# Scores product and fold in two token halves, the maximum ordered between products, new in-order positions, and down weights in row pairs, in a one-core decode block

## The chip, the cores and the metric

The kernel runs on one core of one Trainium2 chip. The metric is device time in microseconds (us) of one execution, smaller is better. The executions of one kernel on one chip agree within about 0.3%; the median over the runs is quoted.

Engines in the profile: PE (TensorE, matrix products; PEld is its weight load), DVE (VectorE), ACT (ScalarE), POOL (GpSimd), SP (SyncE, which here issues all large DMA loads). A "ring" below is one of the 16 parallel streams over which one DMA load is spread. Packet records in the trace show 16 packets in flight at a time.

## The reference, cut to what matters

One decode token passes through an adaLN-conditioned block: layer norm, attention over a key and value cache of 32 heads with 16384 tokens of 128 elements, and then a gated feed-forward part.

```python
q = (h @ wq).reshape(32 heads, 128)
scores = einsum('bhqd,bhkd->bhqk', q, k_cache) * 128 ** -0.5      # 32 x 16384
p = softmax(scores, axis=-1)
o = einsum('bhqk,bhkd->bhqd', p, v_cache)
x = x + ga * (o.reshape(...) @ wo)
h = layernorm(x) * (1 + cb) + sb
x = x + gb * ((silu(h @ w_gate) * (h @ w_up)) @ w_down)           # 640 -> 1728 -> 640
# ... the modulation vectors sa, ca, ga, sb, cb, gb come from silu(c) @ w_mod
```

Each K or V head is 4 MB, so the two caches are 268 MB of the 291 MB that must be read. Nothing is read twice.

## The kernel before

All work is planned as operations with an engine, a position and dependencies. An engine executes its operations in the order of position, strictly. The scores of one head are made without a transposed K: DVE multiplies K (tokens on partitions and along the row) by a broadcast q in place, adds the two halves of the 128 elements ("fold1", 64 left), PE adds those up further against an identity matrix ("fold", 4 left), and DVE reduces the rest.

```python
o_mult[h]  = op(DVE, base, ...)          # kslot[128, 128 tokens, 128] *= q; 128x16384
o_fold1[h] = op(DVE, base + 8.8, ...)    # f1 = kslot[:, :, 0:64] + kslot[:, :, 64:128]
o_fold[h]  = op(PE, base + 13.5, ...)    # 16 products of 512 columns, S_ps = sum over groups of GC = 4
o_red[h]   = op(DVE, base + 17.0, ...)   # S_sb = sum over the last 4
o_max[h]   = op(DVE, base + 19.3, ...)   # pm = max over the row
o_gm[h]    = op(POOL, base + 19.6, ...)  # maximum over partitions
# ... nb, exp on ACT; the next head's product has position base + 20 and waits for nothing but K and q
o_pvlast[h] = op(PE, vbase, f_pv, deps=[o_exp[h], d_v[h][0], ...])   # V product
```

The loads: K and V have two buffers each. K of head h+2 is issued when `fold1` of head h is done; V of head h when the V product of head h-2 is done. All are issued in one fixed order by SP, the last ones being V of head 30, V of head 31 (four pieces), the gate, up and down weights.

```python
vdeps = [o_pvlast[h - 2]] if h >= 2 else [...]
wd_src = B_wd[0:128 * FJ, :].rearrange("(j p) n -> p j n", p=128)   # rows of 640 x 2 B = 1280 B
wd_cut = [(0, 5), (5, 9), None, (9, FJ - 1), (FJ - 1, FJ)]           # five loads, None: the 64 last rows
```

## Time and profile before

| | before |
|---|---|
| median | 690.39 us (690.14 to 691.23, 4 runs) |
| span of the profiled run | 688.9 us |
| bytes read | 290.96 MB, 422 GB/s over the span |
| busy | DVE 66%, PE 49%, POOL 43%, ACT 12%; DMA 90% or more in all slices but the last |

In the profile's lines, kring and vring are the buffers of K and V, f is the result of `fold1`, psb is PSUM (the memory that PE writes its products to), gm is the maximum over partitions, and SPq is SP issuing loads.

From the page of the profile of the kernel before: busy time of the engines; then the span in 40 slices with the DMA's busy tenths and its GB/s; then the chain of work that ended last.

```profile
PE 336.4 (49%) x3320; PEld 173.8 (25%) x3320; DVE 454.4 (66%) x155; ACT 85.3 (12%) x308; POOL 292.9 (43%) x75
...
DMA  9999999999999999999999999999999999999997
GB/s 383 418 427 436 438 433 425 432 428 430 429 425 436 437 430 429 431 430 427 432 433 427 431 429 434 429 434 431 430 427 422 431 440 436 425 426 430 390 370 263
...
DMA 37%; DVE 21%; POOL 18%; PE 17%; SPq 3%; ACT 2%; issue 1%
DMA kring<-in_A_k_cache_dram 36%; POOL gm L439 18%; DVE kring L419 13%; PE psb L429 9%; PE psb L458 7%; DVE f L421 6%; SPq L71 3%; DVE S_sb L433 2%; DMA kring<-in_B_w_down_dram 1%; ACT P_sb L443 1%; DVE pm L436 1%; ACT R_sb L407 1%; PE psb 
```

The DMA row says that the queue is full nearly everywhere, and the GB/s row that it moves about 430 in the middle. A kernel with no hole at 430 GB/s would need 677 us for its bytes. What can be won lies mainly in the start and the last three slices. POOL has 18% of the chain with its maximum (`gm`), although it should be a tiny operation.

From the timeline of the kernel before: one head near the end, where DVE does not wait for K. The columns are start, duration, engine, line, operation, and in brackets the idle time before it with what ended it.

```profile
583.38 8.68 DVE L419 TENSOR_TENSOR kring<-kring,qbc_sb 128x16384 bf16<-128x16384 bf16 x1
583.56 8.72 POOL L439 PARTITION_ALL_REDUCE gm<-pm  x1 [6.33 <-DVE pm L436]
597.29 3.63 PE L429 MATMUL psb<-f,ident 128*128 128x512 bf16 x16
...
600.96 0.69 DVE L433 TENSOR_REDUCE S_sb<-psb 128x128 f32<-128x512 f32 x1 [4.43 <-PE psb L429]
...
601.88 8.68 DVE L419 TENSOR_TENSOR kring<-kring,qbc_sb 128x16384 bf16<-128x16384 bf16 x1
```

The next head's product starts on DVE at 583.38, POOL's maximum 0.2 us later, and POOL ends when the product ends: 8.72 us. The cycle from product to product is 601.88 - 583.38 = 18.5 us here, up to 20.1 in later heads, and 19.2 on average over the last five cycles (product starts from 545.4 to 641.4). A head's K and V need 8.39 MB / 430 GB/s = 19.5 us.

Busy time of each engine in short stretches of the kernel before. The last two columns are the DMA's busy share and GB/s; the one ahead of them is the TensorE clock that the throttle granted (1.00 is full).

```profile
core 0: us, PE busy (x) PEld busy (x) DVE busy (x) ACT busy (x) POOL busy (x), PEclk, DMA share, GB/s
651.00:652.00 1.00, 0.69 (x10) 0.42 (x14) 1.00 (x1) 0.25 (x3) 0.81 (x1) 0.50 0.76 328
652.00:653.00 1.00, 1.00 (x16) 0.46 (x12) 1.00 (x1) 0.00 (x0) 1.00 (x1) 0.50 0.53 229
653.00:654.00 1.00, 1.00 (x16) 0.33 (x12) 1.00 (x1) 0.00 (x0) 1.00 (x1) 0.50 0.30 131
654.00:655.00 1.00, 1.00 (x12) 0.16 (x4) 0.59 (x1) 0.14 (x1) 0.83 (x1) 0.51 0.38 164
655.00:656.00 1.00, 1.00 (x9) 0.43 (x6) 0.00 (x0) 0.78 (x3) 0.00 (x0) 1.00 0.00 0
656.00:657.00 1.00, 1.00 (x6) 0.44 (x5) 0.00 (x0) 0.00 (x0) 0.00 (x0) 1.00 0.76 147
```

This is a hole in the load stream. The last V load is issued at 655.2 us, when the V product of head 29 has ended; that product began at 651.60, right after an exponential that waited for a maximum of 8.7 us (641.62 to 650.33). From the timeline: that exponential (P_sb), the scaled output of a head (On), its output product, the V product, and the last V load.

```profile
650.61 0.40 ACT L443 ACTIVATE P_sb<-S_sb,nb 128x128 bf16<-128x128 f32 x1
...
651.01 0.24 ACT L497 ACTIVATE On<-psb,rl 128x1 bf16<-128x1 f32 x1
...
651.31 0.36 PE L505 MATMUL psb<-On,woring 128*128 128x1 bf16 x5 [10.04 <-ACT On L497]
...
651.60 3.56 PE L458 MATMUL psb<-vring,P_sb 128*32 128x512 bf16 x32
...
655.20 1.99 SPq L71 DMA_DIRECT2D vring<-in_A_v_cache_dram  x4
```

### The profile page before, as it was taken

The numbers are of one execution on the slowest core, as the hardware profiler recorded it, in microseconds if no ns is written. First come the engines' busy times: TensorE is split into PE (matmuls) and PEld (weight loads), VectorE is DVE, ScalarE is ACT, GpSimd is POOL, SyncE is SP. The second block draws the span as 40 slices with busy tenths as digits, with TensorE's granted clock in tenths as the row PEclk, the third lists the DMA queues.
The fourth block names the chain that finished last, engine by engine and source line by source line (L and its number), as shares of the span: only waits on it lengthen the run. The fifth ranks groups of instructions, "written<-read, shape, count | busy, mean of one in ns | idle before, by whom it ended". The sixth has DMA issues, their size and how long they took to land.

```text
span 688.9 us, 7385 instructions
## 1 busy us (share of the span) xinstructions
PE 336.4 (49%) x3320; PEld 173.8 (25%) x3320; DVE 454.4 (66%) x155; ACT 85.3 (12%) x308; POOL 292.9 (43%) x75
## 2 busy tenths in 40 slices
PE   1503455565444445655444455643446256544484
PEld 1501222232122222322122222311223122212253
DVE  0077767667788776656787666667766676778801
ACT  0100101111111111111011111101111011111010
POOL 0006666556677654324055531000054365667600
PEclk9997666667676666667666666666666666766675
DMA  9999999999999999999999999999999999999997
GB/s 383 418 427 436 438 433 425 432 428 430 429 425 436 437 430 429 431 430 427 432 433 427 431 429 434 429 434 431 430 427 422 431 440 436 425 426 430 390 370 263
DMA packets 13613, 290.96 MB, mean 422 GB/s; under 512 B 1354, under 2 KB 3596, under 8 KB 4492
## 3 DMA queue, kind: packets, MB, share of 16 engines
q1 hardware_dynamic: 13576, 290.48, 98.7%
q8 instruction: 26, 0.43, 0.2%
q14 instruction: 7, 0.06, 0.0%
q10 hardware_dynamic: 4, 0.00, 0.0%
HBM read 290.47 MB, written 0.00 MB: 422 GB/s over the span
## 4 chain that ended last, share of the span: by engine, by line
DMA 37%; DVE 21%; POOL 18%; PE 17%; SPq 3%; ACT 2%; issue 1%
DMA kring<-in_A_k_cache_dram 36%; POOL gm L439 18%; DVE kring L419 13%; PE psb L429 9%; PE psb L458 7%; DVE f L421 6%; SPq L71 3%; DVE S_sb L433 2%; DMA kring<-in_B_w_down_dram 1%; ACT P_sb L443 1%; DVE pm L436 1%; ACT R_sb L407 1%; PE psb L410 0%; ACT nb L441 0%; ACT On L497 0%
## 5 line engine op out<-in xcount | busy, mean ns | idle before, releaser
L419 DVE TENSOR_TENSOR kring<-kring,qbc_sb 128x16384 bf16<-128x16384 bf16 x32 | 278.0, 8687 | 28.6 <-DMA kring<-in_A_k_cache_dram 28.6
L439 POOL PARTITION_ALL_REDUCE gm<-pm x32 | 145.1, 4534 | 319.2 <-DVE pm L436 314.2
L458 PE MATMUL psb<-vring,P_sb 128*32 128x512 bf16 x992 | 109.0, 618 | 126.3 <-DMA vring<-in_A_v_cache_dram 126.3
L446 POOL PARTITION_ALL_REDUCE Ls<-rs x32 | 145.0, 4532 | 27.4 <-ACT P_sb L443 27.4
L429 PE MATMUL psb<-f,ident 128*128 128x512 bf16 x512 | 132.1, 414 | 27.8 <-DVE f L421 27.5
L421 DVE TENSOR_TENSOR f<-kring 128x8192 bf16<-128x8192 bf16 x32 | 141.6, 4424 | 1.1
L433 DVE TENSOR_REDUCE S_sb<-psb 128x128 f32<-128x512 f32 x32 | 22.1, 691 | 153.5 <-PE psb L429 153.5
L429 PEld LDWEIGHTS psb<-f,ident 128*128 128x128 bf16 x512 | 50.1, 103 | 117.3 <-DVE f L421 42.1
L458 PEld LDWEIGHTS psb<-vring,P_sb 128*32 128x32 bf16 x992 | 33.7, 138 | 179.8 <-DMA vring<-in_A_v_cache_dram 128.5
L410 PE MATMUL psb<-R_sb,ones_bf 128*128 128x128 bf16 x32 | 8.5, 266 | 126.5 <-ACT R_sb L407 126.5
L478 PEld LDWEIGHTS psb<-sel,acc_sb 128*32 128x32 f32 (+1 forms) x920 | 58.9, 157 | 13.8 <-issue 11.9
L478 PE MATMUL psb<-sel,acc_sb 128*32 128x1 f32 (+1 forms) x920 | 61.2, 200 | 0.7 <-ACT acc_sb L463 0.7
L441 ACT ACTIVATE nb<-gm 128x1 f32<-128x1 f32 x32 | 6.5, 203 | 313.3 <-POOL gm L439 313.3
L410 PEld LDWEIGHTS psb<-R_sb,ones_bf 128*128 128x128 bf16 x32 | 3.3, 104 | 129.5 <-ACT R_sb L407 129.5
L463 ACT ACTIVATE acc_sb<-psb 128x512 f32<-128x512 f32 x31 | 18.5, 596 | 108.8 <-PE psb L458 108.7
L505 PE MATMUL psb<-On,woring 128*128 128x1 bf16 x160 | 8.1, 180 | 41.7 <-ACT On L497 41.7
L448 ACT ACTIVATE lnl<-Ls 128x1 f32<-128x1 f32 x32 | 6.5, 202 | 112.7 <-POOL Ls L446 112.7
L505 PEld LDWEIGHTS psb<-On,woring 128*128 128x128 bf16 x160 | 7.3, 131 | 42.6 <-ACT On L497 42.6
L443 ACT ACTIVATE P_sb<-S_sb,nb 128x128 bf16<-128x128 f32 x32 | 12.8, 402 | 1.2 <-ACT nb L441 0.2
L407 ACT ACTIVATE R_sb<-ident,q_r 128x128 bf16<-128x128 bf16 x32 | 12.7, 397 | 0.6
L413 ACT ACTIVATE qbc_sb<-psb 128x128 bf16<-128x128 f32 x32 | 8.9, 277 | 14.2 <-PE psb L410 14.2
L328 POOL PARTITION_ALL_REDUCE st<-st x2 | 0.8, 392 | 21.7 <-DVE x L529 11.4
(72 smaller groups left out, 88.1 us busy)
## 6 DMA issues: line engine op xcount, KB each, us to landing
kring<-in_A_k_cache_dram SPq DMA_DIRECT2D x32, 4096.0 KB, 25.1
vring<-in_A_v_cache_dram SPq DMA_DIRECT2D x31, 4096.0 KB, 33.0
wreg<-in_A_wq_dram SPq DMA_DIRECT2D x1, 5120.0 KB, 26.6
woring<-in_A_wo_dram SPq DMA_DIRECT2D x8, 640.0 KB, 24.8
vring<-in_w_mod_dram SPq DMA_DIRECT2D x1, 4800.0 KB, 14.6
vring<-in_A_v_cache_dram SPq DMA_DIRECT2D x4, 1024.0 KB, 9.4
wreg<-in_B_w_gate_dram SPq DMA_DIRECT2D x1, 2160.0 KB, 16.5
wreg<-in_B_w_up_dram SPq DMA_DIRECT2D x1, 2160.0 KB, 21.4
```

The lines of the kernel that those rows point to most:

```text
L71: return e.dma_start(out_ap, in_ap)
L407: o_R[h] = op(ACT, base - 15.0 if h > 0 else 2.5, lambda e, h=h, s2=s2: e.activation(out=R_sb[:, s2], in_=ident[:], func=ACTF.Copy, scale= ...
L419: o_mult[h] = op(DVE, base, lambda e, kslot=kslot, qb=qb: e.tensor_tensor(out=kslot, in0=kslot, in1=qb, op=ALU.mult), deps=[d_k[h], o_qbc[ ...
L421: o_fold1[h] = op(DVE, base + 8.8, lambda e, kslot=kslot: e.tensor_tensor(out=f1[:], in0=kslot[:, :, 0:64], in1=kslot[:, :, 64:128], op=AL ...
L429: r = e.matmul(S_ps[s2][:].rearrange("p (t r) -> p t r", r=GC), lhsT=ident[:], rhs=f1[:, :, GC * m:GC * (m + 1)], start=(m == 0), stop=(m ...
L433: o_red[h] = op(DVE, base + 17.0, lambda e, s2=s2: e.tensor_reduce(out=S_sb[:, s2], in_=S_ps[s2][:].rearrange("p (t r) -> p t r", r=GC), a ...
L439: o_gm[h] = op(POOL, base + 19.6, lambda e, h=h: e.partition_all_reduce(gm[:, h:h + 1], pm[:, h:h + 1], channels=128, reduce_op=bass.bass_ ...
L443: o_exp[h] = op(ACT, base + 20.4, lambda e, h=h, s2=s2, sp=sp: e.activation(out=P_sb[:, sp, 0:TT], in_=S_sb[:, s2], func=ACTF.Exp, scale=S ...
L446: o_L[h] = op(POOL, base + 21.0, lambda e, h=h: e.partition_all_reduce(Ls[:, h:h + 1], rs[:, h:h + 1], channels=128, reduce_op=bass.bass_i ...
L458: r = e.matmul(acc_ps[s2][q4:q4 + 32, :], lhsT=P_sb[:, sp, 4 * j:4 * j + 32], rhs=vring[:, s2, 4 * j:4 * j + 4, :].rearrange("p a d -> p ( ...
L463: o_acc[h] = op(ACT, vbase + 9.0, lambda e, s2=s2: e.activation(out=acc_sb[:, s2, :], in_=acc_ps[s2][:], func=ACTF.Copy), deps=[o_pvlast[h ...
L478: r = e.matmul(dst, lhsT=blk, rhs=sel[:, i:i + 1], start=(i == 0), stop=(i == 3))
```

## The change

Its intent: shorten the head's cycle and take the maximum out of the collision with the product. The product and `fold1` are made in two halves of 64 tokens, so that PE folds the first half while DVE multiplies the second; each half has its own bank of PSUM and leaves 8 values (GC = 8) for the reduction; the products of the next head wait for the maximum; small operations of ACT and PE get earlier positions; the down weights come in pairs of neighbouring rows (2560 B), for which the gate and up weights are picked at a stride of two columns.

```diff
-    GC = 4
+    GC = 8
+    NH = 2
-            vbase = base + 10.5 + PERIOD * lead(h)
+            vbase = base + 10.0 + PERIOD * lead(h)
-            o_mult[h] = op(DVE, base, ... 128x16384 ..., deps=[d_k[h], o_qbc[h]])
-            o_fold1[h] = op(DVE, base + 8.8, ...)
-            o_fold[h] = op(PE, base + 13.5, f_fold, ...)
-            o_red[h] = op(DVE, base + 17.0, ...)
+            for c in range(NH):
+                o_mult[h] = op(DVE, base + 6.5 * c, ... 128x8192 ...,
+                               deps=[d_k[h], o_qbc[h], o_gm[h - 1] if h >= 1 else None])
+                o_fold1[h] = op(DVE, base + 6.5 * c + 4.4, ...)
+                o_fold[h].append(op(PE, base + 6.5 * c + 6.7, f_fold, ...))      # 8 products of 512 columns
+                reds.append(op(DVE, base + 15.0 + c, ...))                       # 128x512 -> 128x64
 # ... max, gm, nb, exp, L, lnl, rl: positions about 2 earlier; acc, diag, on, wo: 5 to 6 earlier
+        NPR = FJ // 2
+        wd_cut = [(0, 3), (3, 5), None, (5, NPR), NPR]                            # in row pairs
+                src = B_wd[256 * c[0]:256 * c[1], :].rearrange("(q p i) n -> p q (i n)", p=128, i=2)
 # ... gate and up: w = wv[:, k, 256 * (j // 2):...].rearrange("p (m i) -> p i m", i=2)[:, j % 2, :]
```

More of the change, by code (lines that the diff above doesn't have):

```diff
@@ L215, in build @@
         acc_sb = sb("acc_sb", [128, 2, 512], F32)
-        sel = sb("sel", [128, GC], F32)
+        sel = sb("sel", [128, 4], F32)
         identf = sb("identf", [128, 128], F32)
@@ L271, in build @@
         o_sel = op(DVE, 0.1, lambda e: e.tensor_reduce(
-            out=sel[:], in_=ident[:].rearrange("p (g r) -> p r g", g=4)[:, 0:GC, :], axis=AX.X, op=ALU.add), deps=[o_ident], name="sel")
+            out=sel[:], in_=ident[:].rearrange("p (g r) -> p r g", g=4)[:, 0:4, :], axis=AX.X, op=ALU.add), deps=[o_ident], name="sel")
         o_idf = op(DVE, 0.12, lambda e: e.tensor_copy(out=identf[:], in_=ident[:]), deps=[o_ident], name="identf")
@@ L380, in build @@
         o_R, o_qbcmm, o_qbc = [None] * H, [None] * H, [None] * H
-        o_fold = [None] * H
+        o_fold = [[] for _ in range(H)]
         o_mult, o_fold1, o_red, o_max = [None] * H, [None] * H, [None] * H, [None] * H
@@ L415, in build @@
                 deps=[o_qbcmm[h], o_mult[h - 2] if h >= 2 else None], name="qbc%d" % h)
-            kslot = kring[:, s2]
-            qb = qbc_sb[:, s2].unsqueeze(1).broadcast_to([128, TT, 128])
-            o_mult[h] = op(DVE, base, lambda e, kslot=kslot, qb=qb: e.tensor_tensor(out=kslot, in0=kslot, in1=qb, op=ALU.mult),
-                           deps=[d_k[h], o_qbc[h]], name="mult%d" % h)
-            o_fold1[h] = op(DVE, base + 8.8, lambda e, kslot=kslot: e.tensor_tensor(
-                out=f1[:], in0=kslot[:, :, 0:64], in1=kslot[:, :, 64:128], op=ALU.add),
-                deps=[o_mult[h], o_fold[h - 1] if h >= 1 else None], name="fold1_%d" % h)
@@ L425, in f_fold @@
-            def f_fold(e, s2=s2):
-                r = None
-                n = 64 // GC
-                for m in range(n):
-                    r = e.matmul(S_ps[s2][:].rearrange("p (t r) -> p t r", r=GC), lhsT=ident[:], rhs=f1[:, :, GC * m:GC * (m + 1)],
-                                 start=(m == 0), stop=(m == n - 1))
-                return r
-            o_fold[h] = op(PE, base + 13.5, f_fold, deps=[o_fold1[h], o_ident, (o_modc_a, o_qbf)[h] if h < 2 else o_red[h - 2]], name="fold%d" % h)
@@ L433, in build, with f_fold @@
-            o_red[h] = op(DVE, base + 17.0, lambda e, s2=s2: e.tensor_reduce(
-                out=S_sb[:, s2], in_=S_ps[s2][:].rearrange("p (t r) -> p t r", r=GC), axis=AX.X, op=ALU.add),
-                deps=[o_fold[h], o_exp[h - 2] if h >= 2 else None], name="red%d" % h)
-            o_max[h] = op(DVE, base + 19.3, lambda e, h=h, s2=s2: e.tensor_reduce(
+            TH = TT // NH
+            qb = qbc_sb[:, s2].unsqueeze(1).broadcast_to([128, TH, 128])
+            reds = []
+            for c in range(NH):
+                ks = kring[:, s2, c * TH:(c + 1) * TH, :]
+                f1h = f1[:, c * TH:(c + 1) * TH, :]
+                sh = S_ps[c][:].rearrange("p (t r) -> p t r", r=GC)
+                o_mult[h] = op(DVE, base + 6.5 * c, lambda e, ks=ks, qb=qb: e.tensor_tensor(out=ks, in0=ks, in1=qb, op=ALU.mult),
+                               deps=[d_k[h], o_qbc[h], o_gm[h - 1] if h >= 1 else None], name="mult%d_%d" % (h, c))
+                o_fold1[h] = op(DVE, base + 6.5 * c + 4.4, lambda e, ks=ks, f1h=f1h: e.tensor_tensor(
+                    out=f1h, in0=ks[:, :, 0:64], in1=ks[:, :, 64:128], op=ALU.add),
+                    deps=[o_mult[h], o_fold[h - 1][c] if h >= 1 else None], name="fold1_%d_%d" % (h, c))
+                def f_fold(e, sh=sh, f1h=f1h):
+                    r = None
+                    n = 64 // GC
+                    for m in range(n):
+                        r = e.matmul(sh, lhsT=ident[:], rhs=f1h[:, :, GC * m:GC * (m + 1)], start=(m == 0), stop=(m == n - 1))
+                    return r
+                o_fold[h].append(op(PE, base + 6.5 * c + 6.7, f_fold, deps=[o_fold1[h], o_ident, (o_modc_a, o_qbf)[c] if h < 1 else o_red[h - 1]],
+                                    name="fold%d_%d" % (h, c)))
+                reds.append(op(DVE, base + 15.0 + c, lambda e, s2=s2, sh=sh, c=c: e.tensor_reduce(
+                    out=S_sb[:, s2, c * TH:(c + 1) * TH], in_=sh, axis=AX.X, op=ALU.add),
+                    deps=[o_fold[h][c], o_exp[h - 2] if h >= 2 else None], name="red%d_%d" % (h, c)))
@@ L437, in build @@
+            o_red[h] = reds[-1]
+            o_max[h] = op(DVE, base + 17.0, lambda e, h=h, s2=s2: e.tensor_reduce(
                 out=pm[:, h:h + 1], in_=S_sb[:, s2], axis=AX.X, op=ALU.max), deps=[o_red[h]], name="max%d" % h)
-            o_gm[h] = op(POOL, base + 19.6, lambda e, h=h: e.partition_all_reduce(
+            o_gm[h] = op(POOL, base + 17.3, lambda e, h=h: e.partition_all_reduce(
                 gm[:, h:h + 1], pm[:, h:h + 1], channels=128, reduce_op=bass.bass_isa.ReduceOp.max), deps=[o_max[h]], name="gm%d" % h)
-            o_nb[h] = op(ACT, base + 20.2, lambda e, h=h: e.activation(
+            o_nb[h] = op(ACT, base + 18.0, lambda e, h=h: e.activation(
@@ L442, in build @@
                 out=nb[:, h:h + 1], in_=gm[:, h:h + 1], func=ACTF.Copy, scale=-SCALE), deps=[o_gm[h]], name="nb%d" % h)
-            o_exp[h] = op(ACT, base + 20.4, lambda e, h=h, s2=s2, sp=sp: e.activation(
+            o_exp[h] = op(ACT, base + 18.2, lambda e, h=h, s2=s2, sp=sp: e.activation(
                 out=P_sb[:, sp, 0:TT], in_=S_sb[:, s2], func=ACTF.Exp, scale=SCALE, bias=nb[:, h:h + 1], accum_out=rs[:, h:h + 1]),
                 deps=[o_nb[h], o_red[h], o_pvlast[h - NP] if h >= NP else o_zp], name="exp%d" % h)
-            o_L[h] = op(POOL, base + 21.0, lambda e, h=h: e.partition_all_reduce(
+            o_L[h] = op(POOL, base + 18.6, lambda e, h=h: e.partition_all_reduce(
@@ L447, in build @@
                 Ls[:, h:h + 1], rs[:, h:h + 1], channels=128, reduce_op=bass.bass_isa.ReduceOp.add), deps=[o_exp[h]], name="L%d" % h)
-            o_lnl[h] = op(ACT, base + 30.2, lambda e, h=h: e.activation(
+            o_lnl[h] = op(ACT, base + 28.0, lambda e, h=h: e.activation(
                 out=lnl[:, h:h + 1], in_=Ls[:, h:h + 1], func=ACTF.Ln), deps=[o_L[h]], name="lnl%d" % h)
-            o_rl[h] = op(ACT, base + 30.3, lambda e, h=h: e.activation(
+            o_rl[h] = op(ACT, base + 28.1, lambda e, h=h: e.activation(
@@ L462, in build @@
                 o_pvlast[h] = op(PE, vbase, f_pv, deps=[o_exp[h], d_v[h][0], o_acc[h - 2] if h >= 2 else (o_xf, o_modc)[h], o_cc], name="pv%d" % h)
-                o_acc[h] = op(ACT, vbase + 9.0, lambda e, s2=s2: e.activation(out=acc_sb[:, s2, :], in_=acc_ps[s2][:], func=ACTF.Copy),
+                o_acc[h] = op(ACT, vbase + 3.0, lambda e, s2=s2: e.activation(out=acc_sb[:, s2, :], in_=acc_ps[s2][:], func=ACTF.Copy),
                               deps=[o_pvlast[h], o_diag[h - 2] if h >= 2 else None], name="acc%d" % h)
@@ L479, in f_diag @@
                     return r
-                o_diag[h] = op(PE, vbase + 9.5, f_diag, deps=[o_acc[h], o_sel, o_on[h - 1] if h >= 1 else None], name="diag%d" % h)
+                o_diag[h] = op(PE, vbase + 4.0, f_diag, deps=[o_acc[h], o_sel, o_on[h - 1] if h >= 1 else None], name="diag%d" % h)
             else:
@@ L496, in build @@
                 on_dst, on_src, on_sc = On[qs, h - hq:h - hq + G], OT_ps[qs, h - hq:h - hq + G], rl[qs, h:h + 1]
-            o_on[h] = op(ACT, vbase + 10.0, lambda e, a=on_dst, b=on_src, c=on_sc: e.activation(out=a, in_=b, func=ACTF.Copy, scale=c),
+            o_on[h] = op(ACT, vbase + 5.0, lambda e, a=on_dst, b=on_src, c=on_sc: e.activation(out=a, in_=b, func=ACTF.Copy, scale=c),
                          deps=[o_diag[h], o_rl[h]], name="on%d" % h)
@@ L508, in build @@
             if lastg:
-                o_wo[h] = op(PE, vbase + 10.5, lambda e, h=h: f_wo(e, h, h + 1), deps=[o_on[h], d_wo[h // G], o_gbr], name="wo%d" % h)
+                o_wo[h] = op(PE, vbase + 5.5, lambda e, h=h: f_wo(e, h, h + 1), deps=[o_on[h], d_wo[h // G], o_gbr], name="wo%d" % h)
             elif hq == G - 1:
-                o_wo[h] = op(PE, vbase + 10.5, lambda e, h=h: f_wo(e, h + 1 - G, h + 1), deps=[o_on[h], d_wo[h // G], o_gbr], name="wo%d" % h)
+                o_wo[h] = op(PE, vbase + 5.5, lambda e, h=h: f_wo(e, h + 1 - G, h + 1), deps=[o_on[h], d_wo[h // G], o_gbr], name="wo%d" % h)
         TE = T0 + (H - 1) * PERIOD + 10.5 + PERIOD * lead(H - 1) + 20.0
@@ L516, in build @@
         d_wu = plan.dma(QE + 0.01, wu_v, B_wu.rearrange("(p k) n -> p k n", k=KC), "wu", deps=[o_qmm], name="dma_wu")
-        wd_src = B_wd[0:128 * FJ, :].rearrange("(j p) n -> p j n", p=128)
-        wd_cut = [(0, 5), (5, 9), None, (9, FJ - 1), (FJ - 1, FJ)]
+        NPR = FJ // 2
+        wd_cut = [(0, 3), (3, 5), None, (5, NPR), NPR]
         d_wd = []
@@ L521, in build @@
             if c is None:
-                d_wd.append(plan.dma(QE + 0.02 + 0.01 * n, wdr_v[0:FR], B_wd[128 * FJ:F, :], ("wd", n), deps=[o_fold1[H - 2]], name="dma_wd%d" % n))
-            else:
-                d_wd.append(plan.dma(QE + 0.02 + 0.01 * n, wd_v[:, c[0]:c[1]], wd_src[:, c[0]:c[1]], ("wd", n), deps=[o_fold1[H - 2]], name="dma_wd%d" % n))
+                dst, src = wdr_v[0:FR], B_wd[128 * FJ:F, :]
+            elif c == NPR:
+                dst, src = wd_v[:, 2 * NPR, :], B_wd[256 * NPR:128 * FJ, :]
+            else:
+                dst = wd_v[:, 2 * c[0]:2 * c[1], :].rearrange("p (q i) n -> p q (i n)", i=2)
+                src = B_wd[256 * c[0]:256 * c[1], :].rearrange("(q p i) n -> p q (i n)", p=128, i=2)
+            d_wd.append(plan.dma(QE + 0.02 + 0.01 * n, dst, src, ("wd", n), deps=[o_fold1[H - 2]], name="dma_wd%d" % n))
         o_abf = op(ACT, TE, lambda e: e.activation(out=attn_bf[:], in_=attn_ps[:, 0:KC], func=ACTF.Copy), deps=[o_wo[H - 1]], name="attn_bf")
@@ L537, in build @@
                   deps=[o_t2], name="h2_col")
-        o_zg = op(DVE, TE - 1.0, lambda e: e.memset(g_ps[:, 0:FCH], 0.0), deps=[o_modc_a, o_red[H - 2]], name="zero_g")
+        o_zg = op(DVE, TE - 1.0, lambda e: e.memset(g_ps[:, 0:FCH], 0.0), deps=[o_modc_a, o_red[H - 1]], name="zero_g")
         o_zu = op(DVE, TE - 0.9, lambda e: e.memset(u_ps[:, 0:FCH], 0.0), deps=[o_qbf, o_red[H - 1]], name="zero_u")
@@ L545, in f_gu @@
                 for k in range(KC):
-                    w = wv[:, k, 128 * j:min(F, 128 * (j + 1))]
+                    if j < 2 * NPR:
+                        w = wv[:, k, 256 * (j // 2):256 * (j // 2 + 1)].rearrange("p (m i) -> p i m", i=2)[:, j % 2, :]
+                    else:
+                        w = wv[:, k, 128 * j:min(F, 128 * (j + 1))]
                     r = e.matmul(ps_t[0:(128 if j < FJ else FR), j:j + 1], lhsT=w, rhs=h2_col[:, k:k + 1],
@@ L582, in build @@
         for n, c in enumerate(wd_cut):
-            js = [FJ] if c is None else list(range(*c))
+            js = [FJ] if c is None else ([2 * NPR] if c == NPR else list(range(2 * c[0], 2 * c[1])))
             o_dn = op(PE, TE + 1.8 + 0.01 * n, lambda e, n=n, js=js: f_down(e, js, n == 0, n == len(wd_cut) - 1),
```

## The prediction

> **What bounds it now.** DMA. The page gives 290.96 MB in 688.9 us. In the table by 10 us stretches, every stretch from 10 to 650 us has a DMA share of 0.97 to 1.05 and about 430 GB/s; the packet records show 16 packets in flight throughout, a 32 KB one taking 1.215 us. At that rate all bytes need 676 us, so 13 us are losable: start-up (1.6), one hole, slow small packets with rings out of step, and the end (3.9 us after the last landing). DVE is busy 66% only.
>
> **The hole.** By 1 us stretches, the DMA share falls to 0.76, 0.53, 0.30, 0.38, 0.00, 0.76 from 651 to 657 us. The last V load is issued at 655.2, when the V product of head 29 ends (timeline). That was late because the chain of waits holds, from 539 on, a cross-partition maximum of 8.7 us per head: POOL starts it 0.2 us after the next 8.68 us product on DVE and ends with it; alone it takes 0.35 us. The Trainium skill, "SBUF — State Buffer", section "SBUF: two separate sides", describes an exclusive shared port pair; 8.7 against 0.35 us agree.
>
> **What the change does.**
> - Maximum before the next product: POOL 8.7 -> about 0.4 us; a DVE pause of about 0.7 us instead.
> - Product and fold in halves: DVE 2 x 4.35 and 2 x 2.2 us (same sum). PE's first half fold hides under DVE, leaving a wait of 2 us, not 4.4 to 5.5. The reduction reads twice as much PSUM: +0.69 us a head. Compute-bound head cycle about 17 us, not 18.5 to 20; the bytes take 19.5.
> - So near the end compute follows K's landing rather than trailing by 8 us; the V product of head 29 ends near 646 us (estimate), before the V of head 30 has landed (651 to 655.6 by ring). The hole should vanish.
> - Down weights: 1280 B packets take 58 ns. From the 1280 B and 32 KB durations the fixed part is about 10.5 ns, so a 2560 B packet takes about 105 ns (estimate): 6.3 us a ring become 5.8. Gate and up weights are loaded at stride 2: some 0.5 us more on PE, mostly hidden.
>
> **How much counts.** The hole averages 3.2 to 3.7 us over the rings, but the slowest ring stood idle only from 655.6 to 656.2, and the end is set by the slowest ring. It then needs 9.9 (V) + 10.3 (gate, up) + 5.8 us: landing near 682 instead of 685.0, unless rings drift apart further. I expect 3.2 us gained: 690.5 -> **687.3 us, 685.0 to 690.0**. Chances: faster by over 2% 0.01, within 2% 0.98, slower 0.01.
>
> **What would show each step.** Maximum about 0.4 us in every head, POOL busy from 293 to under 150 us; DVE busy about 475; DMA share near 1.0 from 646 to 677, last V issued by about 647; 2560 B packets near 105 ns; rate in the middle unchanged; last down-weight landing near 682, then 3.5 to 4 us.
>
> **What would make it wrong.** The V product of head 29 waiting in PE's fixed order, so that a hole stays (no gain); rings drifting more without the hole's resynchronisation (gain 1 to 2); strided weight loads making PE the tail's limit (gain 2); a late V blocking the half fold behind it, delaying K issues (costs some us).

## The result

The changed kernel takes 688.53 us (688.53 to 688.56, 4 runs) against 690.39 us: 1.9 us less. The ratio is 0.9971, with a 95% interval of 0.9954 to 0.9988. Ratios in this document are the mean time of one kernel's fast runs over that of the other's of the same rounds, so not quite the ratio of the medians. The time is inside the predicted range; the forecast gain was 3.2 us.

From the page of the profile after, the parts that answer to those shown of before:

```profile
PE 350.9 (51%) x3320; PEld 174.7 (25%) x3320; DVE 482.4 (70%) x251; ACT 81.5 (12%) x308; POOL 51.3 (7%) x75
...
GB/s 387 409 434 427 433 434 435 426 433 430 431 420 441 430 427 428 430 429 434 431 433 430 430 427 431 427 434 428 433 436 418 438 428 428 428 429 430 425 421 238
...
DMA 51%; DVE 41%; PE 6%; ACT 1%; issue 1%; SPq 1%; POOL 0%; DVEq 0%
```

POOL's busy time fell from 292.9 to 51.3 us, DVE's rose from 454.4 to 482.4. POOL is gone from the chain. The three last GB/s figures were 390, 370, 263 and are 425, 421, 238: two slices are full now, and the last one is emptier.

From the timeline after, one head at a place where DVE does not wait for K:

```profile
544.97 4.43 DVE L425 TENSOR_TENSOR kring<-kring,qbc_sb 128x8192 bf16<-128x8192 bf16 x1 [0.57 <-POOL gm L446]
...
551.63 4.42 DVE L425 TENSOR_TENSOR kring<-kring,qbc_sb 128x8192 bf16<-128x8192 bf16 x1
...
551.77 3.59 PE L435 MATMUL psb<-f,ident 128*128 128x512 bf16 x8 [5.54 <-DVE f L427]
...
556.09 2.29 DVE L427 TENSOR_TENSOR f<-kring 128x4096 bf16<-128x4096 bf16 x1
...
558.43 1.90 PE L435 MATMUL psb<-f,ident 128*128 128x512 bf16 x8 [1.04 <-DVE f L427]
...
561.48 0.35 POOL L446 PARTITION_ALL_REDUCE gm<-pm  x1 [11.85 <-DVE pm L443]
561.96 4.43 DVE L425 TENSOR_TENSOR kring<-kring,qbc_sb 128x8192 bf16<-128x8192 bf16 x1 [0.57 <-POOL gm L446]
```

The maximum takes 0.35 us; the first half's fold (551.77, PE) lies beneath DVE's second half; the cycle is 561.96 - 544.97 = 17.0 us, as predicted. The 8 products of the first half take 3.59 us and those of the second 1.90. PE had been idle for 5.5 us before the first ones. The Trainium skill, "TensorE: Matmul & The Clock Gate", section "Part 1: The HAM clock gate (the "warmup" mystery)", says that an idle window of about 3.4 us puts the array back to half its clock; 449 against 238 ns a product agree, and so does the granted clock: 0.50 from 551.8 to 555.3 us, 1.00 from 558.5 to 560.3.

The short stretches after; first the place where the hole was, then the end of the loads:

```profile
651.00:652.00 1.00, 1.00 (x7) 0.42 (x5) 0.00 (x0) 0.00 (x0) 0.00 (x0) 1.00 0.84 352
652.00:653.00 1.00, 1.00 (x10) 0.97 (x8) 0.61 (x1) 0.00 (x0) 0.00 (x0) 1.00 0.93 393
653.00:654.00 1.00, 0.49 (x7) 0.33 (x6) 0.79 (x6) 0.39 (x2) 0.35 (x1) 1.00 0.82 336
654.00:655.00 1.00, 0.00 (x0) 0.00 (x0) 0.00 (x0) 0.57 (x3) 0.30 (x1) 0.86 1.08 442
...
679.00:680.00 1.00, 0.01 (x1) 0.00 (x0) 0.17 (x1) 0.00 (x0) 0.00 (x0) 0.50 0.64 248
680.00:681.00 1.00, 0.73 (x24) 0.66 (x24) 0.00 (x0) 0.00 (x0) 0.00 (x0) 0.50 0.55 209
681.00:682.00 1.00, 0.45 (x16) 0.21 (x12) 0.00 (x0) 0.00 (x0) 0.00 (x0) 0.50 0.23 86
682.00:683.00 1.00, 0.79 (x20) 0.27 (x12) 0.00 (x0) 0.00 (x0) 0.00 (x0) 0.50 0.12 34
```

The V product of head 29 and the last V load, after:

```profile
647.31 2.17 PE L465 MATMUL psb<-vring,P_sb 128*32 128x512 bf16 x32
...
649.53 1.75 SPq L71 DMA_DIRECT2D vring<-in_A_v_cache_dram  x4
```

The hole is gone but for a dip: the last V load is issued at 649.5 us, when the V product of head 29 has ended, and the first rings run out of the V before it at about 651.5. From 651 to 657 us 0.5 us of the DMA's share is missing (lowest 0.80), against 3.3 before. But from 679 on the share falls to 0.64, 0.55, 0.23, 0.12: some rings have finished, others have not. In the packet records the last down-weight packet ends at 685.0 us before and 682.7 after. From there to the end of the span it is 3.9 us before and 4.1 after.

### The profile page after: what moved, and what is told of

Its sections match the earlier page's. It is cut to its first block, busy times and chain, and to the rows that moved or that the text cites. A ratio compares the mean times of both kernels' runs of the same rounds, so it can differ in the third digit from the quotient of the medians.

```text
span 686.8 us, 7505 instructions
## 1 busy us (share of the span) xinstructions
PE 350.9 (51%) x3320; PEld 174.7 (25%) x3320; DVE 482.4 (70%) x251; ACT 81.5 (12%) x308; POOL 51.3 (7%) x75
## 4 chain that ended last, share of the span: by engine, by line
DMA 51%; DVE 41%; PE 6%; ACT 1%; issue 1%; SPq 1%; POOL 0%; DVEq 0%
DMA kring<-in_A_k_cache_dram 46%; DVE kring L425 26%; DVE f L427 14%; DMA kring<-in_B_w_down_dram 4%; PE psb L435 3%; PE psb L485 1%; SPq L71 1%; DVE S_sb L439 0%; ACT P_sb L450 0%; PE psb L465 0%; PE psb L594 0%; ACT R_sb L408 0%; POOL gm L446 0%; ACT qbc_sb L414 0%; PE psb L411 0%
## 5 line engine op out<-in xcount | busy, mean ns | idle before, releaser
L425 DVE TENSOR_TENSOR kring<-kring,qbc_sb 128x8192 bf16<-128x8192 bf16 x64 | 283.0, 4422 | 94.4 <-DMA kring<-in_A_k_cache_dram 70.0
L435 PE MATMUL psb<-f,ident 128*128 128x512 bf16 x512 | 177.6, 510 | 255.0 <-DVE f L427 254.9
L427 DVE TENSOR_TENSOR f<-kring 128x4096 bf16<-128x4096 bf16 x64 | 146.7, 2292 | 2.2
L439 DVE TENSOR_REDUCE S_sb<-psb 128x64 f32<-128x512 f32 x64 | 44.0, 688 | 52.4 <-PE psb L435 52.4
L465 PE MATMUL psb<-vring,P_sb 128*32 128x512 bf16 x992 | 75.0, 455 | 9.2 <-DMA vring<-in_A_v_cache_dram 9.2
L446 POOL PARTITION_ALL_REDUCE gm<-pm x32 | 11.2, 351 | 533.4 <-DVE pm L443 515.3
L465 PEld LDWEIGHTS psb<-vring,P_sb 128*32 128x32 bf16 x992 | 26.6, 111 | 64.6 <-DMA vring<-in_A_v_cache_dram 28.1
L453 POOL PARTITION_ALL_REDUCE Ls<-rs x32 | 37.3, 1164 | 48.8 <-ACT P_sb L450 48.8
L504 ACT ACTIVATE On<-psb,rl 32x4 bf16<-32x4 f32 (+1 forms) x32 | 8.2, 256 | 125.4 <-PE psb L485 120.7
L443 DVE TENSOR_REDUCE pm<-S_sb 128x1 f32<-128x128 f32 x32 | 9.2, 286 | 1.1
```

The lines of the kernel that those rows point to most:

```text
L425: o_mult[h] = op(DVE, base + 6.5 * c, lambda e, ks=ks, qb=qb: e.tensor_tensor(out=ks, in0=ks, in1=qb, op=ALU.mult), deps=[d_k[h], o_qbc[h] ...
L427: o_fold1[h] = op(DVE, base + 6.5 * c + 4.4, lambda e, ks=ks, f1h=f1h: e.tensor_tensor(out=f1h, in0=ks[:, :, 0:64], in1=ks[:, :, 64:128], ...
L435: r = e.matmul(sh, lhsT=ident[:], rhs=f1h[:, :, GC * m:GC * (m + 1)], start=(m == 0), stop=(m == n - 1))
L439: reds.append(op(DVE, base + 15.0 + c, lambda e, s2=s2, sh=sh, c=c: e.tensor_reduce(out=S_sb[:, s2, c * TH:(c + 1) * TH], in_=sh, axis=AX. ...
L446: o_gm[h] = op(POOL, base + 17.3, lambda e, h=h: e.partition_all_reduce(gm[:, h:h + 1], pm[:, h:h + 1], channels=128, reduce_op=bass.bass_ ...
L453: o_L[h] = op(POOL, base + 18.6, lambda e, h=h: e.partition_all_reduce(Ls[:, h:h + 1], rs[:, h:h + 1], channels=128, reduce_op=bass.bass_i ...
```

## The experiments

All kernels gave correct results. "Before" beside each run is the kernel before.

| run | what | chip | this, us | before, us | ratio (95%) |
|---|---|---|---|---|---|
| after | the change | - | 688.53 | 690.39 | 0.9971 (0.9954 to 0.9988) |
| e1 | before + row pairs | 0 | 690.92 | 691.05 | 0.9999 (0.9986 to 1.0013) |
| e2 | after, no row pairs | 0 | 688.93 | 691.05 | 0.9969 (0.9956 to 0.9983) |
| e3 | before + order of the maximum | 0 | 719.70 | 691.05 | 1.0416 (1.0402 to 1.0430) |
| e4 | after, no order of the maximum | 0 | 688.86 | 691.05 | 0.9968 (0.9955 to 0.9982) |
| e5 | after + all rings stopped once | 8 | 691.51 | 691.25 | 1.0005 (0.9990 to 1.0021) |
| e6 | after + six down loads | 8 | 689.15 | 691.25 | 0.9971 (0.9957 to 0.9985) |
| e7 | after + tiny marking loads | 8 | 690.25 | 691.25 | 0.9987 (0.9972 to 1.0003) |
| e8 | e6 + up weights in two | 9 | 688.73 | 690.81 | 0.9969 (0.9956 to 0.9981) |
| e9 | e8 + 13 rows a partition | 9 | 688.85 | 690.81 | 0.9971 (0.9958 to 0.9983) |
| e10 | after, old positions | 9 | 688.70 | 690.81 | 0.9967 (0.9954 to 0.9981) |
| e11 | after again | 9 | 689.01 | 690.81 | 0.9970 (0.9957 to 0.9984) |
| e12 | e7 again, one look | 4 | 690.26 | 690.78 | - |

### Which part of the change removed the hole (e1 to e4, e10)

**e1**: the row pairs alone.

```diff
 (kernel before)
-        wd_cut = [(0, 5), (5, 9), None, (9, FJ - 1), (FJ - 1, FJ)]
+        wd_cut = [(0, 3), (3, 5), None, (5, NPR), NPR]     # and the strided gate and up weights
```

> The kernel before with the down weights in row pairs alone. My theory (the end is set by the slowest DMA ring; a 2560 B packet takes 102 to 105 ns against two of 58): the hole at 651 to 657 us stays, the last landing comes about 0.5 to 0.7 us earlier, time 689.6 to 690.0 against 690.4 before. Rival (most of the change's 1.9 us came from the row pairs, since the down weights are the last thing to land): 1.2 us or more, 689.2 or less.

Measured: no difference (0.9999), less than either theory said. The packets did get faster (2560 B in 104 ns, as against two of 58), and the hole stayed; the last packet ended at 684.8 us, 0.2 earlier than in the kernel before. The first down product started at 682.30, and from 683.89 on PE multiplied the rest one after another. Whether PE or the loads kept the time is not separated here.

**e2**: the change without the row pairs.

```diff
 (kernel after)
-        wd_cut = [(0, 3), (3, 5), None, (5, NPR), NPR]
+        wd_cut = [(0, 5), (5, 9), None, (9, FJ - 1), (FJ - 1, FJ)]   # single rows, gate and up at stride 1
```

> The changed kernel with the down weights as before (single rows of 1280 B). My theory: the hole is gone and the scores part keeps about 1.4 us of the 1.9; time 688.9 to 689.3. Rival (row pairs bring most of the gain): 690.0 or more.

Measured: 688.93 us, as my theory said. On the same chip it is 2.1 us below the kernel before and within 0.1 us of e4, which has the pairs. The scores part brings the gain; that the pairs bring anything is not seen.

**e3**: the order of the maximum alone, with whole products.

```diff
 (kernel before)
-                           deps=[d_k[h], o_qbc[h]], name="mult%d" % h)
+                           deps=[d_k[h], o_qbc[h], o_gm[h - 1] if h >= 1 else None], name="mult%d" % h)
```

> The kernel before, with one dependency more: each product waits until the maximum of the head before is done. Whole products, no halves, no pairs. My theory (the blocked maximum alone delays the V product of head 29, and with it the last V load): each maximum about 0.35 us, the last V load issued near 646 instead of 655.2 us, no hole, time 689.0 to 689.6, DMA share near 1 up to 676. Rival (the halves are needed, since DVE then waits for both fold and maximum, a head cycle of 19.5 us or more): the hole stays in part, time 690.2 or more.

Measured: 719.7 us, 4.2% slower. My theory fell, and more deeply than the rival had it. From the timeline of e3, one head in the middle:

```profile
304.24 8.69 DVE L419 TENSOR_TENSOR kring<-kring,qbc_sb 128x16384 bf16<-128x16384 bf16 x1 [0.58 <-POOL gm L439]
...
317.45 5.65 PE L429 MATMUL psb<-f,ident 128*128 128x512 bf16 x16 [9.37 <-DVE f L421]
...
323.13 0.69 DVE L433 TENSOR_REDUCE S_sb<-psb 128x128 f32<-128x512 f32 x1 [5.74 <-PE psb L429]
...
324.24 0.35 POOL L439 PARTITION_ALL_REDUCE gm<-pm  x1 [11.06 <-DVE pm L436]
...
324.72 8.69 DVE L419 TENSOR_TENSOR kring<-kring,qbc_sb 128x16384 bf16<-128x16384 bf16 x1 [0.58 <-POOL gm L439]
```

The maximum takes 0.35 us as hoped. But the cycle is 324.72 - 304.24 = 20.48 us, and a head's bytes take 19.5: DVE paces every head, and 31 cycles at about 1 us too long are the 29 us. Of the cycle, 5.74 us is DVE waiting for PE's fold (4.8 on average in the kernel before), and 0.58 is the new wait for the maximum. The fold takes 5.65 us here; PE stood idle for 9.4 us before it, and its granted clock is 0.62 on average from 317 to 323 us. In the kernel before, the V product came late, just ahead of the fold, and kept PE running: the fold of 597.29 above follows a V product at a granted clock of 1.00 and takes 3.63 us (4.1 on average over all heads). So the blocked maximum had a use: what it delayed kept PE at a higher clock.

**e4**: the change without the order.

```diff
 (kernel after)
-                               deps=[d_k[h], o_qbc[h], o_gm[h - 1] if h >= 1 else None], name="mult%d_%d" % (h, c))
+                               deps=[d_k[h], o_qbc[h]], name="mult%d_%d" % (h, c))
```

> The changed kernel without the new dependency: halves and pairs, the maximum may again collide with the next product's first half. My theory: a collided maximum takes about 4.4 us, but at the end DVE waits for K anyway, so that the last V load is still issued before 651 us; time as the changed kernel, 688.3 to 688.9. Rival (the order is what removes the hole): the hole is back, time 690 or more.

Measured: 688.86 us, as my theory said: the order is not needed. The group of the maximum in e4, with its mean over all 32 heads:

```profile
L446 POOL PARTITION_ALL_REDUCE gm<-pm x32 | 35.8, 1120 | 530.3 <-DVE pm L443 512.7 <-DVE psb L553 17.5
```

On average 1.12 us: it collides only where DVE is behind K, and then with half a product (at most 4.5 us). Elsewhere DVE waits for K and POOL has it to itself. The last V load went out at 649.83 us and there was no hole.

**e10**: the change with the old in-order positions.

```diff
 (kernel after)
-            vbase = base + 10.0 + PERIOD * lead(h)
+            vbase = base + 10.5 + PERIOD * lead(h)
-            ... acc, diag, on, wo at vbase + 3.0, 4.0, 5.0, 5.5
+            ... acc, diag, on, wo at vbase + 9.0, 9.5, 10.0, 10.5   # and gm, nb, exp, L, lnl, rl as before
```

> The changed kernel with the in-order positions of the kernel before for the small operations of ACT and the V products. My theory: the order on ACT is off the critical path, within 0.3 us of e11. Rival (the positions are a part of what removes the hole): the hole returns in part, 0.5 us or more slower than e11.

Measured: 688.70 us against 689.01 of e11 on the same chip, no slower. With the halves and the order in place, the new positions are not needed.

Together, by elimination: the halves (with GC = 8) do it. Pairs, order and positions were each left out once, and the hole stayed away. With halves the cycle drops clearly below the 19.5 us of the bytes, with the order (17.0 us) and without it (16.3 us in e4, from product to product at 544.29 and 560.62), where the kernel before had 19.2 on average; so DVE catches up with K and the V product of head 29 comes early enough.

Two kernels that would test this were not run: the halves alone, and the new positions alone in the kernel before. The second is a rival. In the kernel before, `On` of head 28 is planned 0.1 behind the exponential of head 30; the change plans it 3.2 ahead of it. That alone might have let the V product of head 29 start when its V had landed (646.4), without halves. Whether the hole would have gone, or PE would have started the folds at a low clock as in e3, no run shows.

### Where the rest of the hole went (e5, e7, e12)

In the hole before, the missing shares of the six stretches sum to 0.24 + 0.47 + 0.70 + 0.62 + 1.00 + 0.24 = 3.3 us (of which 0.5 is still missing after). The gain was 1.9.

**e5**: all rings are made to stop and start together once.

```diff
 (kernel after)
-            vdeps = [o_pvlast[h - 2]] if h >= 2 else [...]
+            vdeps = [o_pvlast[h - 2]] + (d_v[h - 1] if h == H - 1 else []) if h >= 2 else [...]
```

> The changed kernel with one dependency more: the last V load waits until the V load before it has landed on all rings, so that all 16 rings stand still for a moment and start again together, as in the hole of the kernel before. My theory (the end is set by the slowest ring, and the hole cost only what the slowest ring stood idle): the rings' spread at the last landing falls from some 6 us to about 2, the slowest ring loses the 1.5 to 2.5 us of receipt, issue and first byte; time 690.0 to 691.3. Rival (rings do not matter, only mean idle time of the queue): the mean idle of a full stop, over 4 us with the spread of 4.5 us at 651, is added: 692.5 or more.

Measured: 691.51 us, 2.4 us above e6 on the same chip (e6 differs little from the changed kernel, below), just above the range that my theory gave and below the rival's. The stop in e5:

```profile
654.00:655.00 1.00, 0.00 (x0) 0.00 (x0) 0.00 (x0) 0.54 (x3) 0.34 (x1) 1.00 0.37 147
655.00:656.00 1.00, 0.00 (x0) 0.00 (x0) 0.00 (x0) 0.41 (x2) 0.05 (x1) 1.00 0.00 0
656.00:657.00 1.00, 0.61 (x12) 0.36 (x16) 0.00 (x0) 0.00 (x0) 0.00 (x0) 0.93 0.00 0
```

Missing shares from 651 to 659 sum to 0.16 + 0.47 + 0.47 + 0.63 + 1 + 1 + 0.33 + 0.18 = 4.2 us, and 2.4 us reached the time. I read the rest as fallen on rings that would have stood idle at the end anyway. The spread shows in the packet records: for each load, the time from its first packet's start to its last packet's end, less the mean work per ring. For the up and gate weights this is 12.0 - 10.3 = 1.7 us in e5, 2.0 in the kernel before, and 4.4 after.

**e7**: marking loads, to see which ring is where.

```diff
 (kernel after)
+        for nt, vh in enumerate((15, H - 1)):          # ahead of V of head 15, and of head 31
+            for j in range(1, 17):
+                n = 4 + 2 * j                          # distinct sizes: 12 to 72 bytes
+                d_tag = plan.dma(qpos["v", vh] - 0.5 + 0.01 * j, tag[0:j, tc:tc + n], A_wq[0:j, tc:tc + n], ...)
```

A load over j partitions uses the lowest j rings, as the Trainium skill has it ("DMA: Bandwidth & Descriptors", section "Why a DMA increments its semaphore by 16 and not by 1"). The records agree as far as they can: j packets of each size were seen. Ring j-1 is then the one that first shows up with size j; I followed the rings from size to size by nearest time.

> The changed kernel with two sets of 16 tiny extra loads (1 to 16 partitions, 12 to 72 bytes each), one ahead of the V load of head 15 and one ahead of the last. By the Trainium skill's page on DMA a load over j partitions runs on the lowest j rings, so the sizes tell which ring is where. Time as the changed kernel plus at most 0.5 us. My theory (some rings are always slower): the same rings are behind at both places, and the lag about doubles, from about 2.5 to about 4.5 us. Rival (random drift): the order of the rings differs between the two places.

**e12**: the same kernel on another chip, for its profile.

> The kernel of e7 again, for its profile alone, by chance on another chip. My theory (each ring has its own steady rate): rings 7, 8 and 15 ahead and rings 5, 6, 13 and 14 more than 3 us behind at the last V load, as in e7, with a spread of 4 to 5.5 us. Rival (the lag belongs to one execution or one chip): another order.

Start of the last marking packet on each ring, in us after the first ring's, reconstructed from the packet records (not a view of the profile):

```
ring               0    1    2    3    4    5    6    7    8    9   10   11   12   13   14   15
e7  ahead of V15  1.3  1.9  1.5  2.2  0.6  3.1  3.1  0.4  0.0  1.7  1.7  2.1  1.7  3.8  3.4  0.1
e7  ahead of V31  2.1  3.8  2.4  3.3  1.4  4.7  4.6  0.3  0.1  3.7  3.6  2.3  1.8  3.9  3.5  0.0
e12 ahead of V31  2.1  4.2  2.6  4.1  1.3  4.9  4.6  0.3  0.0  3.8  3.6  2.3  2.2  3.9  3.6  0.1
```

The same rings lag on two chips, by nearly the same amounts, and the order at 652 us is much that at 343 us: rings 7, 8 and 15 are ahead and rings 5 and 6 last. But "each ring has its own steady rate" is wrong, as the packet and semaphore records of the kept traces show. All rings move a 32 KB packet in about 1.22 us, and from 60 to 520 us, in the kernels before and after, the order and distance of their landings stay the same from load to load, to about 0.1 us, until one ring falls back at a step. Each step goes with a packet of a queue that the profile calls instruction. From the page of the kernel before (queue, packets, MB, share):

```profile
q8 instruction: 26, 0.43, 0.2%
```

One step: a ring's load packet ends at 231.15 us; a 16 KB instruction packet runs from 231.15 to 232.16; the ring's next load packet starts at 232.15 and takes 1.76 us instead of 1.22. So this ring lost about 1.5 us, and the spread of the landings went from 2.2 to 3.1 us. From 60 to 510 us there were 19 such packets (four of them 8 KB, of another instruction queue), and the lags of all rings behind the first grew by 26 us in sum. e7 and e12 have 15 each between the two marks. That the same program sends them over the same rings each time, and so the same rings lag on two chips, fits but was not followed by ring number. The marks cost more than expected: e7 is 1.1 us slower than e6.

That is why a hole is worth less than it looks. In the hole the fast rings waited for the slow ones; without it they run on and wait at the end. The slowest ring had stood idle for little of the hole: the last one ended its V at 655.7, and all started again from 656.2 to 656.9. These 0.5 to 1.2 us do not give the whole 2.3 us by which the last packet came earlier. The row pairs may give up to 0.5 (an estimate from their packet times), and the instruction packets after 656 us put the last ring back by 1.4 us before (spread 0.5 to 1.9) and by 1.0 after (4.5 to 5.5). The remainder is open.

### What limits the end (e6, e8, e9, e11)

**e6**: six down loads instead of five.

```diff
 (kernel after)
-        wd_cut = [(0, 3), (3, 5), None, (5, NPR), NPR]
+        wd_cut = [(0, 2), (2, 4), None, (4, 5), (5, NPR), NPR]
```

> The changed kernel with the down weights in six loads instead of five, two row pairs in each of the first two. My theory: after the last landing PE still has 0.8 us of products that waited for large loads; with smaller ones the last product starts on landing; time 687.7 to 688.2 against 688.5. Rival (the last landing alone sets the end): within 0.2 us of the changed kernel.

Measured: ratio 0.9971, the same as the changed kernel; no gain is seen. From the timeline of e6, the up product, the product of the two with the gate, and the first and last down products:

```profile
678.29 2.25 PE L563 MATMUL psb<-h_col,wreg 128*128 128x1 bf16 x70 [4.33 <-DMA wreg<-in_B_w_up_dram]
680.64 0.17 DVE L572 TENSOR_TENSOR gu_col<-psb,sg 128x14 bf16<-128x14 f32 x1 [5.78 <-PE psb L563]
...
680.87 0.70 PE L594 MATMUL psb<-kring,gu_col 128*1 128x160 bf16 x16 [0.34 <-DVE gu_col L572]
...
684.27 0.30 PE L594 MATMUL psb<-kring,gu_col 128*1 128x160 bf16 x4 [0.17 <-PE psb L594]
```

Behind the landing of the up weights PE has a chain of its own of 684.57 - 678.29 = 6.3 us at half clock, about as long as the down weights need to land. Finer loads cannot shorten it.

**e11** is the yardstick for the next two:

> The changed kernel itself once more, as the yardstick for the three others on their chip: ratio to the kernel before 0.996 to 0.998.

Measured: ratio 0.9970, as expected.

**e8**: also the up weights in two loads.

```diff
 (e6)
-        d_wu = plan.dma(QE + 0.01, wu_v, ...)
+        d_wu = [...]        # rows 0 to 2 and 3 to 4 of each partition's five
-        o_u = op(PE, TE + 1.25, lambda e: f_gu(e, wu_v, u_ps), deps=[o_h2, d_wu, o_zu], name="up")
+        o_u = op(PE, TE + 1.25, lambda e: f_up(e, 0, KU), deps=[o_h2, d_wu[0], o_zu], name="up0")
+        o_u = op(PE, TE + 1.26, lambda e: f_up(e, KU, KC), deps=[o_u, d_wu[1]], name="up1")
```

> The changed kernel with six down-weight loads (as in e6) and with the up weights in two loads, three fifths and two fifths, each multiplied when it lands. My theory (after the fine cuts failed): behind the up weights' landing PE has a chain of 6.5 us of its own, as long as the rest of the DMA, so that neither alone moves the end; with 1.3 us taken from PE's chain the last landing sets the end: 0.6 to 0.9 us less than the changed kernel of the same call, ratio about 0.9990. Rival (the last landing alone): no difference from e11.

Measured: 688.73 us (688.68 to 689.12) against 689.01 (688.81 to 689.10). That is 0.3 us and the ranges overlap; I expected 0.6 to 0.9. The theory missed: PE's chain did start earlier (first down product at 679.60), but then the second load of down weights landed only at about 681.2, on the slowest ring, and 2.8 us of products were still to do.

**e9**: 13 neighbouring rows on each partition.

```diff
 (e8)
-                src = B_wd[256 * c[0]:256 * c[1], :].rearrange("(q p i) n -> p q (i n)", p=128, i=2)
+        wd_src = B_wd[0:128 * FJ, :].rearrange("(p j) n -> p j n", j=FJ)
+                        w = wv[:, k, 0:128 * FJ].rearrange("p (m j) -> p j m", j=FJ)[:, j, :]   # stride 13
```

> As e8, with 13 neighbouring rows of the down weights on each partition, loaded in packets of 2560 to 5120 B instead of 2560 and 1280 B. My theory: some 0.25 us a ring less, estimated from 104 ns for 2560 B, 55 for 1280 and 199 for 5120; 0.2 to 0.5 us less than e8. Rival (weight loads at stride 13 cost PE more than that): more than e8.

Measured: 688.85 us (688.78 to 689.50) against 688.73 (688.68 to 689.12) of e8: the gain of the theory is not seen, and the difference is too small for the rival. But the rival's cause is there. The weight load and the product of the gate, in e9 and then in the changed kernel (mean ns after the comma):

```profile
L563 PE MATMUL psb<-h_col,wreg 128*128 128x1 bf16 x65 | 4.1, 199 | 2.2 <-DMA wreg<-in_B_w_gate_dram 2.2
...
L563 PEld LDWEIGHTS psb<-h_col,wreg 128*128 128x128 bf16 x65 | 4.0, 159 | 2.3 <-DVE h_col L549 2.3
```

```profile
L563 PE MATMUL psb<-h_col,wreg 128*128 128x1 bf16 x130 | 3.9, 165 | 4.6 <-DMA wreg<-in_B_w_up_dram 2.5 <-DVE h_col L549 1.9 <-issue 0.2
...
L563 PEld LDWEIGHTS psb<-h_col,wreg 128*128 128x128 bf16 x130 | 3.7, 104 | 4.9 <-DMA wreg<-in_B_w_up_dram 2.6 <-DVE h_col L549 2.0 <-issue 0.3
```

At stride 2 a weight load takes 104 ns, as at stride 1 before; at stride 13 it takes 159, and 70 products take 4.42 us (the gate in e9) instead of 2.24 (the up weights in the changed kernel). The Trainium skill, "Advanced Engine Details and Errata", section "SBUF Cachelines", gives lines of 16 bytes and asks for two accesses to each: two columns of 2 bytes apart stay within a line, 13 columns do not, which agrees.

No version here clearly beats the changed kernel.

## Why the prediction was right or wrong, point by point

- **The bound (right).** DMA bounds both kernels; the rate in the middle is unchanged (a 32 KB packet takes 1.215 us in both), and only the end moved.
- **The hole would vanish (right).** It did, by a smaller margin than thought: the V product of head 29 ended at 649.5 us, not 646. It could not have: V of head 29 had landed on all rings only at 646.7, and in PE's order the product stood behind the first half fold of head 31, whose K reached DVE only at 637.0. The first ring ran out of V at about 651.5.
- **Which part removes it (wrong).** The step "That was late because the chain of waits holds, from 539 on, a cross-partition maximum of 8.7 us per head" named the visible wait, and the order of the maximum came first among the remedies. The wait was real, but it reached the V product through the fixed order of ACT and PE, which the prediction named only as a risk. The order alone costs 29 us (e3), and the change without it is as fast (e4). The shorter cycle through halves is what is left (by elimination, see above). I had costed the halves, but not the order alone; with the mean fold wait of the kernel before it would have given about 19.5 us a cycle (an estimate: 20.48 less the 0.93 by which the fold wait grew), at the limit, and PE's low clock put it over.
- **The size of the gain (right in range, 1.9 instead of 3.2 us).** The mis-sized term is the slowest ring's landing, "near 682 instead of 685.0, unless rings drift apart further". It came at 682.7, with 5.3 us between the first ring's last landing and the last ring's; the last step, at 676.5 us, had put the last ring 1.0 us further back (4.5 to 5.5). The steps come with the instruction packets (above), so the spread goes on growing where nothing stops the fast rings. The end after the last packet took 0.2 us longer.
- **The row pairs.** The packet time was right (104 ns for "about 105"), but not "6.3 us a ring become 5.8" as a gain in time: e1 and e2 showed none.
- **Strided weight loads, "some 0.5 us more on PE" (wrong).** At stride 2 they cost nothing: 104 ns and 2.24 us, as before.
- **DVE and POOL (right in kind).** POOL fell to 51 us ("under 150"), further because the sum over partitions also meets an idle DVE now; DVE rose to 482 us ("about 475"). The Trainium skill's exclusive port pair ("SBUF — State Buffer", section "SBUF: two separate sides") fits the traces: 8.7 us beside a whole product, at most 4.5 beside a half, 0.35 alone.

## What to carry to other kernels

When a load stream is full, ask first whether the compute cycle of a head is clearly shorter than its bytes take: 19.2 us against 19.5 left a hole here, 17.0 and 16.3 did not. A visible long wait in the chain can be removed at a loss if the cycle grows with it (4.2% here). Where engines execute in a fixed order, look for what stands between the wait and the late operation: here the V product waited for another head's operations, not for its own inputs. A hole in the load stream can be worth less than its mean (3.3 us missing, 1.9 gained), because the fast DMA rings only move their waiting to the end. Before ordering a small operation ahead of a large one, look at what the delay had kept running: here a late V product had kept PE at full clock for the fold.

## What the Trainium skill lacked or had wrong

- "DMA: Bandwidth & Descriptors", section "Latency and other measured facts", calls engines 7 and 15 usually slower than the others (and guesses that this belongs to loads issued from GpSimd). Here, with loads issued from SP, rings 7, 8 and 15 are the furthest ahead and 5 and 6 the furthest behind, by 4.6 to 4.9 us after 652 us, on two chips (e7, e12), if the lowest rings are numbered as that page says. They are not faster: every ring takes about 1.22 us for a 32 KB packet.
- The same page says that the engines finish independently, but not by how much a long stream of equal loads drifts apart, 3.5 to 3.8 us at 343 us and 4.7 to 4.9 at 652 us, nor what it comes from here: each 16 KB packet of the instruction queue, one in 25 to 30 us, sets one ring back by about 1.5 us.
- The same page, section "Specifications", lists about 358 GB/s as the HBM limit of a core. Read alone this misleads: this one-core program read 430 GB/s for 600 us (422 to 424 over the whole span). A note further down that page says that its measured figures (425 GB/s for 16 MB) are for a core whose neighbour is idle, and that 358 is for both streaming.
- "TensorE: Matmul & The Clock Gate" gives no time for weight loads at a column stride: 104 ns at strides 1 and 2, 159 ns at stride 13 (e9).
